# Attention and mixture of experts in one kernel: another written order for the attention stage

## The chip, the cores and the metric

The kernel runs on one NeuronCore of a Trainium2 chip. Five engines matter: PE (TensorE: matmuls and transposes, with PEld its weight loads), DVE (VectorE), ACT (ScalarE), POOL (GpSimd) and SP (SyncE, which here only issues DMAs). Each works through its own list of instructions in order; a DMA is issued by SP or POOL and lands later. The metric is the time of one execution in device microseconds (us); lower is better. A run is timed three times.

## The reference, cut to what matters

Inputs: `q`, `k`, `v` of shape (4 batches, 8 heads, 768 positions, 64), gates of 512 x 8, and eight experts `w1` (512 x 1024) and `w2` (1024 x 512), all float32.

```python
k_sum = k.reshape(B, H, 24, 32, 64).max(axis=3)       # one summary key per 32 positions
v_sum = v.reshape(B, H, 24, 32, 64).mean(axis=3)
scores = [scale * q @ k.T where |i - j| < 16 else -1e9,  scale * q @ k_sum.T + log(32)]
a = softmax(scores);  x = (a @ [v, v_sum]) -> (3072 tokens, 512)
logits = x @ w_gate;  e = argmax(logits)
out[t] = softmax(logits)[e] * sigmoid(x @ w_output_gate)[e] * (relu(x[t] @ w1[e]) @ w2[e])
```

## The kernel before, in words

The first stage is attention, over 24 tiles of 128 positions (6 per batch). The second is the expert stage: tokens of one expert are gathered in slots of 256 and put through two layers of matmuls. Attention is recorded by hand (`tc.manual_schedule` over all five engines): the order in which `attention` calls its helpers is the order on every engine, and the framework only adds semaphore waits. So a wait of one instruction holds up everything written behind it on its engine.

Before the tiles, `load` brings 256 positions of q or k by DMA from SP, `reorder` copies them into another layout, `prep_k` and `prep_q` turn them on PE (`transposed`) and ACT copies them from PSUM into `kt` and `qt`. `load_vw` brings v into `vw`, in windows of 64 positions with a halo, two DMAs per window; `means` and `gather_means` make the block means of v on PE, `put_means` copies them into `vw` on POOL. `k_sum` copies the block maxima `km` into `kt`. `clear` zeroes parts of `kt` and `vw`.

The loop over tiles runs with a lead of `AHEAD` = 2: iteration i writes `scores(i+2)` (PE `sp`, then DVE adds the mask, `pr`), `exps(i+1)` (ACT), `values` and `norm` of the tiles in `at[i]` (PE `pv`, DVE `xs`), `turn_p(i)` (PE `pt`, ACT copies to `pT`), `smallest(i+2)` (DVE `mn`), loads, the work in `todo`, `put_means`, `store_x` (POOL writes `xs` to DRAM), `subtract(i+2)` (POOL) and `turn_x` (PE `xtr`, ACT `xT`). `HELD` = 4 makes `values` begin in iteration 5, two tiles per iteration until they trail by one tile. Once the last tile of a batch is there, `logits` and `turn_logits` (PE `lp`, `lt`) and `route` follow: `route` finds the expert of each token and the place in the list of that expert, and writes the lists with six indirect DMAs from POOL (`l_dr`, one per tile, each behind a small MEMSET `gap`). After batch 1 `early_slots` computes the first three slots, and `fetch_list` and `fetch` gather their lists (`lst`) and tokens (`xg`), also by indirect DMA from POOL. In iterations 18 to 23 `late_work` adds the loading (SP) and splitting (ACT, DVE) of the first expert's weights.

PSUM has eight banks, which the kernel holds as four tags of two: S for scores, PT for `pt`, PV for `pv`, and TR for everything else.

```python
    for i, (b, tok) in enumerate(tiles):
        if i + AHEAD < n:
            scores(i + AHEAD)
        if i + 1 < n:
            exps(i + 1)
        for t in at[i]:
            values(t)
            norm(t)
        turn_p(i)
```

Of the kernel before, what the change touches and what calls it, by code (L numbers as in the profile page):

```python
# [30 lines left out]
BUFS = {"mn": 4, "pr": 3, "pTe": 4, "pTl": 3, "xs": 3, "den": 3, "xT": 2, "ls": 2, "rawk": 3, "rawq": 2, "natk": 2, "natq": 1}  # L31
# [4 lines left out]
HELD = 4  # L36
# [4 lines left out]
WARM = 44  # L41
# [25 lines left out]
C_SUM = C_AVG + 3 * 32  # L67
# [4 lines left out]
def constants():  # L72

    c = np.zeros((P, C_END), np.float32)
    q = np.arange(P)[:, None]
    col = np.arange(W)
    rel = 64 * (q // 64) + np.where(col < LW, col - PAD, col - PAD - NS)[None, :]
    is_sum = ((col >= LW) & (col < LW + NS))[None, :]
    for t in range(3):
        ok = np.abs(q - rel) < 16  # L80
        if t == 1:
            ok &= rel >= 0
        if t == 2:
# [8 lines left out]
    c[:, C_SEL:C_SEL + 2 * E] = p[:, None] % 32 == np.arange(2 * E)[None, :]  # L92
    for m in range(3):
        for half in range(2):
            row = PAD + 32 * half + np.arange(32)
            c[np.where(row < LW, row, row + NS), C_AVG + 32 * m + 2 * m + half] = 1.0 / 32.0
    for j in range(NS):
        c[32 * (j // 6) + j % 6, C_SUM + j] = 1.0
    return c


def body(tc, q, k, v, w_gate, w_ogate, w1, w2, ident, cst, out):
    nc = tc.nc
    with (
# [22 lines left out]
        with tc.manual_schedule(engines=ALL):  # L127
            for event in attention(tc, const, sa, sb, st, ps, dr, q, k, v, id_sb, c_sb, wg_sb, x_dr, l_dr, rt, late_work):
                if event == "routed":
                    moe.add_slots(early_slots(tc, const, c_sb, rt))  # L130
                    for s in range(EARLY):
                        moe.fetch_list(s, 2)
# [4 lines left out]
                else:  # L137
                    tail = event[1]
# [46 lines left out]
def attention(tc, const, sa, sb, st, ps, dr, q, k, v, id_sb, c_sb, wg_sb, x_dr, l_dr, rt, late_work):  # L185
# [6 lines left out]
    def clear(i):  # L192
# [5 lines left out]
        nc.gpsimd.memset(VW[i][LW:LW + NS, :, :, 0:D], 0.0)  # L198

    def evac(dst, src, scale=None, engine="a"):  # L200
        if engine == "v":
            nc.vector.tensor_copy(dst, src)
        else:
            nc.scalar.activation(dst, src, AF.Copy, scale=1.0 if scale is None else scale)

# [20 lines left out]
    def load_vw(b, tok):  # L226
        for blk in (2 * tok, 2 * tok + 1):
            t = VW[b % 2][:, blk]
            lo = PAD if blk == 0 else 0
            n = PAD if blk == NB - 1 else 32  # L230
            s0 = 64 * blk - PAD
            nc.sync.dma_start(t[lo:LW, :, 0:D], v[b, :, s0 + lo:s0 + LW, :].rearrange("h s d -> s h d"))
            nc.sync.dma_start(t[LW + NS:LW + NS + n, :, 0:D], v[b, :, s0 + LW:s0 + LW + n, :].rearrange("h s d -> s h d"))

    def means(b, m):
        if m == 0:
            msp[0] = ps.tile([P, H * D], F32, name=f"ms{b}", tag="TR", bufs=PB["TR"])
        for j in range(4):
            nc.tensor.matmul(msp[0][32 * j:32 * j + 32],
                             lhsT=c_sb[0:W, C_AVG + 32 * m:C_AVG + 32 * m + 32],  # L240
                             rhs=VW[b % 2][:, 3 * j + m, :, 0:D], start=m == 0, stop=m == 2)
        if m == 2:
            evac(MT.rearrange("p h d -> p (h d)"), msp[0])

    def gather_means(b):
        mg = ps.tile([P, H * D], F32, name=f"mg{b}", tag="TR", bufs=PB["TR"])
# [10 lines left out]
    ms, msp, km = {}, [None], {}  # L257
    first_tags = ["TR", "TR", "S", "S", "PT", "PT", "PV", "PV"]

    def transposed(kind, b, u, g):  # L260
        n = nat[kind, b, u]
        tag = first_tags.pop(0) if first_tags else "TR"
        pt = ps.tile([P, 2, 256], F32, name=f"{kind}tr{b}{u}{g}", tag=tag, bufs=PB[tag])
# [35 lines left out]
    def scores(i):  # L299
# [3 lines left out]
        sp = [ps.tile([P, HP, P], F32, name=f"sp{b}{tok}{x}", tag="S", bufs=PB["S"]) for x in range(2)]  # L303
# [28 lines left out]
    def turn_p(i):  # L332
# [5 lines left out]
        for x in range(2):  # L338
            pt = ps.tile([W, HP, P], F32, name=f"pt{b}{tok}{x}", tag="PT", bufs=PB["PT"])
# [4 lines left out]
    def values(i):  # L344
# [3 lines left out]
        for g in range(2):  # L348
            po = ps.tile([P, 4, D + 1], F32, name=f"pv{b}{tok}{g}", tag="PV", bufs=PB["PV"])
# [18 lines left out]
    def store_x(i):  # L368
        b, tok = tiles[i]
        n0 = b * S + tok * P  # L370
        nc.gpsimd.dma_start(x_dr[n0:n0 + P, :], xss[i].rearrange("p h d -> p (h d)"))

    def turn_x(i):
        b, tok = tiles[i]
        xs = xss.pop(i)
        xp = ps.tile([P, NC, P], F32, name=f"xtr{b}{tok}", tag="TR", bufs=PB["TR"])
# [6 lines left out]
    def logits(b, tok):  # L383

        lp = ps.tile([P, 2 * P], F32, name=f"lp{b}{tok}", tag="TR", bufs=PB["TR"])
# [6 lines left out]
    def turn_logits(b, tok):  # L392
        lt = ps.tile([P, 2, 2 * E], F32, name=f"lt{b}{tok}", tag="TR", bufs=PB["TR"])
# [8 lines left out]
    def route(b):  # L402
# [22 lines left out]
        rk = ps.tile([P, TB + 1, E], F32, name=f"rk{b}", tag="TR", bufs=PB["TR"])  # L425
# [3 lines left out]
        tot = ps.tile([P, E], F32, name=f"tot{b}", tag="TR", bufs=PB["TR"])  # L429
# [8 lines left out]
        posi = tmp("posi", [P, TB], I32)  # L438
        nc.vector.tensor_copy(posi, pos)

# [15 lines left out]
        for t in range(TB):  # L456
            nc.gpsimd.memset(rt["gap"], 0.0)
# [9 lines left out]
    def route_to(b):  # L467

        if b not in routes:
            routes[b] = route(b)  # L470
            next(routes[b])
        else:
            for _ in routes[b]:
                pass
# [4 lines left out]
    for s in range(2):  # L479
        load("q", *steps[s])  # L480
    for tok in range(TB):
        load_vw(0, tok)
    for u in range(3):
        load("k", 1, u)
    for u in range(3):
        reorder("k", 0, u, "vav"[u])
        for g in range(2):
            prep_k(0, u, g)
    reorder("q", 0, 0, "a")
    for g in range(2):  # L490
        prep_q(0, 0, g)
    k_sum(0, "v")
    load("q", *steps[2])
    reorder("q", 0, 1, "p")
    load("q", *steps[3])
    for g in range(2):
        prep_q(0, 1, g)
# [12 lines left out]
    todo = {}  # L510

    def later(i, work):
        todo.setdefault(i, []).append(work)

    for b in range(B):
        first = live[TB * b]
        if b == 0:
            later(first - 2, lambda: [means(0, m) for m in range(3)])
            later(first - 1, lambda: gather_means(0))
        else:  # L520
            later(first - 3, lambda b=b: [means(b, m) for m in range(2)])
            later(first - 2, lambda b=b: means(b, 2))
            later(first - 1, lambda b=b: gather_means(b))
    for s in range(2, len(steps)):
        for g in range(2):
            later(2 * s - 4, lambda s=s, g=g: prep_q(*steps[s], g))
    for b in range(1, B):
        for tok, gs in ({1: (0, 1), 2: (2, 3), 3: (4, 5)} if b == 1 else {0: (0,), 1: (1, 2, 3), 2: (4,), 3: (5,)}).items():
            for x in gs:
                later(TB * (b - 1) + tok, lambda b=b, x=x: prep_k(b, x // 2, x % 2))  # L530
# [5 lines left out]
    exps(0)  # L536
    reorder("q", *steps[2], "p")
    load("q", *steps[4])
    for i, (b, tok) in enumerate(tiles):

        if i + AHEAD < n:
            scores(i + AHEAD)
        if i + 1 < n:
            exps(i + 1)
# [7 lines left out]
        if i == 0:  # L552
            clear(1)
        if i % 2 == 1 and (i + 5) // 2 < len(steps):
            reorder("q", *steps[(i + 5) // 2])
            if (i + 9) // 2 < len(steps):
                load("q", *steps[(i + 9) // 2])
        for kb in range(1, B):
            u = {TB * (kb - 1) + x: y for y, x in enumerate((1, 2, 3) if kb == 1 else (-1, 0, 2))}.get(i)
            if u is not None:  # L560
                reorder("k", kb, u)
            for u in {TB * (kb - 2) + 3: (0, 1), TB * (kb - 2) + 4: (2,)}.get(i, ()) if kb > 1 else ():
                load("k", kb, u)
            t = i - (0 if kb == 1 else TB * (kb - 1) - 1)
            if 0 <= t < TB:
                load_vw(kb, t)
        for x in todo.pop(i, []):
            x()
        for t in range(n):
            if live[t] == i + 1:  # L570
                put_means(*tiles[t])
        if tok == 3 and b + 1 < B:
            k_sum(b + 1)
        for t in at[i]:
            store_x(t)
# [12 lines left out]
        if i == live[2 * TB - 1] + 3:  # L588
            yield "routed"
        if i == live[3 * TB - 1]:  # L590
            yield "last batch"
# [3 lines left out]
    for i in sorted(todo):  # L595
        for x in todo[i]:
            x()
    b, tok = tiles[-1]
    yield "tiles done", [lambda: (values(n - 1), norm(n - 1), store_x(n - 1)), lambda: turn_x(n - 1), lambda: logits(b, tok),
                         lambda: (turn_logits(b, tok), route_to(b)), lambda: route_to(b)]  # L600


def slot_tables(tc, const, c_sb, name, n, t, r):
# [9 lines left out]
    while sft < V:  # L613
# [3 lines left out]
        sft *= 2  # L617
    sh = [P, n, V]
# [13 lines left out]
    rowi = tmp("rowi", [P, 2, n], I32)  # L632
    es, esi = tmp("es", [P, n]), tmp("esi", [P, n], I32)
# [11 lines left out]
    return [([rowi[:, t2, s:s + 1] for t2 in range(2)], esi[0:1, s:s + 1]) for s in range(n)], inc, exc  # L645


def early_slots(tc, const, c_sb, rt):
# [8 lines left out]
    slots, inc, exc = slot_tables(tc, const, c_sb, "a", EARLY, t, base)  # L657
# [7 lines left out]
    return slots  # L665
# [23 lines left out]
class Experts:  # L689
# [133 lines left out]
    def start(self, late_work):  # L823

        self.fetch(0, 2)
# [165 lines left out]
```

## Time and profile before

| | us |
|---|---|
| median of three runs (630.93 to 634.79) | 633.65 |
| profiled execution | 635.28 |
| its span, from the first to the last instruction | 633.5 |
| first matmul of tile scores starts | 27.41 |
| first matmul of the expert stage starts | 282.46 |

In the profiled execution the granted clock of PE is 0.883 of full on average; it is 0.78 from 27.40 to 282.46 us and 0.97 behind that. PE is busy for 169.13 us of the 255.06 us between those two points, and for 330.13 us of the 351.04 us after them. The profile is read as follows: a row of the timeline has a start, a busy time, engine and line, operation with output and inputs, the number of instructions, and in brackets how long the engine was idle before and what ended that idle time. Between start and start of two neighbouring rows of one engine lies what the work really took, since PE's rows overlap a little.

### The profile page before, as it was taken

The page shows a single profiled execution, that of the slowest core. Times are in us where ns is not written, and L with a number is a line of the kernel's source. Part 1 is how long each engine was busy: PE and PEld are TensorE (multiplying, and loading weights), DVE is VectorE, ACT ScalarE, POOL GpSimd, SP SyncE. Part 2 cuts the span into 40 slices and gives each one's busy share as a digit, 9 for nine tenths or more (in the row PEclk, how much of TensorE's full clock was granted, in tenths as well). Part 3 has the DMA queues.
Part 4 walks back from the last instruction along what each step waited for, and adds up shares of the span by engine and source line. Part 5 has one row for each costly group of instructions (what it writes and reads, how often), then busy time and mean ns, then how long its engine had stood idle before and what let it go on. Part 6 is the DMA issues. An engine that isn't in the chain of part 4 may idle for free. (4 is left out here: it accounts for less than half of the span.)

```text
span 633.5 us, 12710 instructions
## 1 busy us (share of the span) xinstructions
PE 513.2 (81%) x4368; PEld 428.7 (68%) x4368; DVE 363.6 (57%) x798; ACT 310.0 (49%) x604; POOL 271.4 (43%) x310
## 2 busy tenths in 40 slices
PE   4668777874870796189999999999999999997992
PEld 4456455642660565079888899889889889885661
DVE  4444534462563257358955775675665765764883
ACT  2326425441650255156544664665554655654782
POOL 7085744527634775460477245353441321211111
PEclk7557969995985798589998999999999999997997
DMA  9966755261743013148286674686585584455881
GB/s 234 179 163 133 167 137 116 85 151 30 164 105 76 25 53 120 47 161 298 80 284 209 225 270 152 229 229 234 209 251 208 209 284 168 168 197 186 298 315 66
DMA packets 108563, 109.51 MB, mean 173 GB/s; under 512 B 46238, under 2 KB 70974, under 8 KB 108480
## 3 DMA queue, kind: packets, MB, share of 16 engines
q1 hardware_dynamic: 99344, 88.96, 46.9%
q0 software_dynamic: 9136, 19.56, 9.8%
q8 instruction: 38, 0.62, 0.4%
q14 instruction: 45, 0.37, 0.2%
HBM read 97.51 MB, written 13.59 MB: 175 GB/s over the span
## 5 line engine op out<-in xcount | busy, mean ns | idle before, releaser
L810 PE MATMUL hp<-xhl,w1h 128*128 128x256 f32 x384 | 109.2, 285 | 0.6 <-DVE xhl L794 0.6
L811 PE MATMUL hp<-xhl,w1l 128*128 128x256 f32 x384 | 108.9, 285 | 0.0
L809 PE MATMUL hp<-xhl,w1h 128*128 128x256 f32 x384 | 107.8, 285 | 1.4 <-ACT xhl L793 1.4
L779 ACT ACTIVATE w2h<-raw 128x512 fp32r<-128x512 f32 x104 | 63.9, 630 | 64.2 <-PE yp L905 23.1
L780 DVE TENSOR_TENSOR w2l<-raw,w2h 128x512 fp32r<-128x512 f32 x104 | 69.4, 687 | 38.9 <-ACT w2h L779 33.6
L903 PE MATMUL yp<-w2h,hh 128*128 128x512 f32 x216 | 86.8, 402 | 0.2 <-ACT hh L873 0.2
L904 PE MATMUL yp<-w2l,hh 128*128 128x512 f32 x216 | 85.2, 394 | 0.0
L905 PE MATMUL yp<-w2h,hl 128*128 128x512 f32 x216 | 84.9, 396 | 0.2
L746 POOL DMA_INDIRECT xg<-x_dr,lst x28 | 34.1, 1219 | 105.4 <-PE xp L791 100.1
L809 PEld LDWEIGHTS hp<-xhl,w1h 128*128 128x128 f32 x384 | 73.6, 193 | 3.0 <-ACT xhl L793 1.9
L810 PEld LDWEIGHTS hp<-xhl,w1h 128*128 128x128 f32 x384 | 74.3, 193 | 1.8 <-DVE xhl L794 0.8
L811 PEld LDWEIGHTS hp<-xhl,w1l 128*128 128x128 f32 x384 | 74.3, 194 | 0.0
L780 DVE TENSOR_TENSOR w1l<-raw,w1h 128x512 fp32r<-128x512 f32 x104 | 66.0, 688 | 9.3 <-ACT w1h L779 8.1
L314 DVE TENSOR_TENSOR pr<-sp,c_sb 128x480 f32<-128x480 f32 x48 | 29.3, 652 | 69.2 <-PE sp L309 65.5
L813 DVE SCALAR_TENSOR_TENSOR hl<-hp,hh 128x256 fp32r<-128x256 f32 x96 | 39.5, 421 | 43.4 <-ACT hh L812 43.2
L330 ACT ACTIVATE pr<-pr 128x960 f32<-128x960 f32 x24 | 24.1, 1003 | 79.4 <-POOL pr L326 78.2
L812 ACT ACTIVATE hh<-hp 128x256 fp32r<-128x256 f32 x96 | 36.4, 380 | 52.7 <-PE hp L811 50.6
L352 PE MATMUL pv<-vw,pT 120*64 120x65 f32 x768 | 35.1, 251 | 30.5 <-POOL vw L255 25.0
L779 ACT ACTIVATE w1h<-raw 128x512 fp32r<-128x512 f32 x104 | 57.5, 620 | 4.6 <-PE hp L810 3.9
L352 PEld LDWEIGHTS pv<-vw,pT 120*64 120x64 f32 x768 | 30.9, 162 | 36.1 <-POOL vw L255 27.5
L309 PE MATMUL sp<-kt,qt 64*64 64x120 f32 x768 | 35.8, 334 | 20.2 <-POOL kt L288 18.5
L326 POOL TENSOR_TENSOR pr<-pr,mn 128x960 f32<-128x960 f32 x24 | 42.9, 1788 | 14.1 <-DVE mn L321 13.2
(298 smaller groups left out, 965.0 us busy)
## 6 DMA issues: line engine op xcount, KB each, us to landing
raw<-in_moe_w_dram SPq DMA_DIRECT2D x208, 256.0 KB, 5.2
raw_k<-in_k_dram SPq DMA_DIRECT2D x12, 512.0 KB, 6.0
raw_q<-in_q_dram SPq DMA_DIRECT2D x12, 512.0 KB, 4.4
x_dr<-xs POOLq DMA_DIRECT2D x24, 256.0 KB, 3.8
vw<-in_v_dram SPq DMA_DIRECT2D x44, 128.0 KB, 4.5
vw<-in_v_dram SPq DMA_DIRECT2D x44, 64.0 KB, 4.0
lst<-l_dr,rowib POOLq DMA_INDIRECT x34, 4.3
xg<-x_dr,lst POOLq DMA_INDIRECT x28, 4.6
```

The lines of the kernel that those rows point to most:

```text
L326: nc.gpsimd.tensor_tensor(pr, pr, mns.pop(i).unsqueeze(2).to_broadcast([P, H, W]), ALU.subtract)
L352: nc.tensor.matmul(po[64 * y:64 * y + 64, h % 4, :], lhsT=pT[:, h % 2, h // 2, 64 * y:64 * y + 64], rhs=VW[b % 2][:, 2 * tok + y, h, 0:D + ...
L779: nc.scalar.activation(hi, raw, AF.Copy)
L780: nc.vector.tensor_tensor(lo, raw, hi.bitcast(F32), ALU.subtract)
L809: nc.tensor.matmul(hp, lhsT=w_h[:, fs], rhs=self.xh[:, c, :], start=c == 0, stop=False)
L810: nc.tensor.matmul(hp, lhsT=w_h[:, fs], rhs=self.xl[:, c, :], start=False, stop=False)
L811: nc.tensor.matmul(hp, lhsT=w_l[:, fs], rhs=self.xh[:, c, :], start=False, stop=c == NC - 1)
L812: nc.scalar.activation(hh[:, j, :], hp, AF.Relu)
L813: nc.vector.scalar_tensor_tensor(hl[:, j, :], hp, 0.0, hh[:, j, :].bitcast(F32), ALU.max, ALU.subtract)
L903: nc.tensor.matmul(y, lhsT=hh[:, j, tk], rhs=w_h, start=j == 0, stop=False)
L904: nc.tensor.matmul(y, lhsT=hh[:, j, tk], rhs=w_l, start=False, stop=False)
L905: nc.tensor.matmul(y, lhsT=hl[:, j, tk], rhs=w_h, start=False, stop=j == NF - 1)
```

## The change

Line numbers of the changed kernel are higher by 3 to 27. The parts:

- All uses of PSUM take the next of four tags in turn (`bank`), so the eight banks go round in the order in which they are written.
- `route` is a generator with more stops: three phases, each in an iteration of its own, and then one stop per indirect DMA. For batch 0 one DMA is written per iteration, for batches 1 and 2 three per iteration. `early_slots` is spread over three iterations, and the lists of the first three slots are fetched in iterations 19, 20 and 21 instead of all in one. The tokens of slot 0 are fetched from `late_work`, in iteration 19.
- `HELD` is 2: `values` begins in iteration 3. The means of batch 0 come in iteration 2, and `means` is one call of 13 matmuls instead of three parts of 4.
- `store_x` is issued by SP instead of POOL, at the start of the next iteration.
- `exps(i+1)` is written behind `turn_p(i)` and the work in `todo`.
- k of later batches is reordered by ACT instead of POOL. `clear(1)` moves ahead of the tiles, and the large MEMSET of `vw` shrinks from 12 windows to one. Half of batch 0's `load_vw` DMAs are issued by POOL. Reordering and turning of q is moved by an iteration.

```diff
-BUFS = {"mn": 4, "pr": 3, "pTe": 4, "pTl": 3, "xs": 3, ...
+BUFS = {"mn": 4, "pr": 3, "pTe": 2, "pTl": 3, "xs": 4, ...
-HELD = 4
+HELD = 2
-WARM = 44
+WARM = 64
-        nc.gpsimd.memset(VW[i][LW:LW + NS, :, :, 0:D], 0.0)
+        nc.gpsimd.memset(VW[i][LW:LW + NS, NB - 1, :, 0:D], 0.0)
+    turn = itertools.cycle(("TR", "S", "PT", "PV"))
+    def bank(shape, name):
+        tag = next(turn)
+        return ps.tile(shape, F32, name=name, tag=tag, bufs=PB[tag])
...
-        sp = [ps.tile([P, HP, P], F32, name=f"sp{b}{tok}{x}", tag="S", bufs=PB["S"]) for x in range(2)]
+        sp = [bank([P, HP, P], f"sp{b}{tok}{x}") for x in range(2)]
...
-        nc.gpsimd.dma_start(x_dr[n0:n0 + P, :], xss[i].rearrange("p h d -> p (h d)"))
+        nc.sync.dma_start(x_dr[n0:n0 + P, :], xss.pop(i).rearrange("p h d -> p (h d)"))
...
         for t in range(TB):
+            yield
             nc.gpsimd.memset(rt["gap"], 0.0)
...
-        reorder("k", 0, u, "vav"[u])
+        reorder("k", 0, u, "vap"[u])
...
+    for tok in range(TB):
+        load_vw(0, tok, (1,), nc.gpsimd)
+    reorder("q", *steps[0], "v")
...
     for i, (b, tok) in enumerate(tiles):
+        for t in at[i - 1] if i else ():
+            store_x(t)
         if i + AHEAD < n:
             scores(i + AHEAD)
-        if i + 1 < n:
-            exps(i + 1)
         for t in at[i]:
             values(t)
             norm(t)
         turn_p(i)
...
-        for x in todo.pop(i, []):
+        for x in early.pop(i, []) + todo.pop(i, []):
             x()
+        if i + 1 < n:
+            exps(i + 1)
...
-                reorder("k", kb, u)
+                reorder("k", kb, u, "a")
...
+                later(i + 4, lambda tb=tb: route_to(tb))
+                for x in range(TB):
+                    later(i + 5 + x // (1 if tb == 0 else 3), lambda tb=tb: scatter(tb), put)
-        if i == live[2 * TB - 1] + 3:
-            yield "routed"
+        if live[2 * TB - 1] + 7 <= i < live[2 * TB - 1] + 7 + EARLY:
+            yield "list", i - live[2 * TB - 1] - 7
```

Three places in the written order follow; `pr15` is the score tile of batch 1, tile 5, and the brackets give the semaphores that an instruction waits for (DMASW: a DMA issued by POOL).

POOL before, at the lists of batch 0, behind the subtraction for tile 5 of batch 1 (three of the six DMAs and the rows behind them):

```order
L326 TENSOR_TENSOR pr15_1280<-pr15_1280,mn15_1322 128x960
L457 MEMSET gap_135 128x1
L458 DMA l_dr_75<-pair0_1507,posi0_1493 24704x2 [waits DMASW7_49,DVE_49]
...
L458 DMA l_dr_75<-pair0_1507,posi0_1493 24704x2 [waits DMASW3_49]
L457 MEMSET gap_135 128x1 [waits Pool_49]
L458 DMA l_dr_75<-pair0_1507,posi0_1493 24704x2 [waits DMASW4_49]
L255 COPY vw1_150<-mst1_1062 24x8x64 [waits DMASW3_49,DMASW2_49,DMASW4_49,DMASW1_49,DMASW7_49,DMASW0_49,Pool_49]
L255 COPY vw1_150<-mst1_1062 24x8x64
L371 DMA x_dr_74<-xs13_1424 128x512 [waits DMASW5_49]
L326 TENSOR_TENSOR pr20_1402<-pr20_1402,mn20_1444 128x960 [waits PE_49,Activation_49,Pool_49]
```

POOL in the changed kernel, at the first two of those DMAs, two and three tiles later:

```order
L471 DMA l_dr_75<-pair0_1503,posi0_1395 24704x2 [waits DMASW2_49,DVE_49]
L338 TENSOR_TENSOR pr21_1544<-pr21_1544,mn21_1585 128x960 [waits DVE_49,PE_49,Activation_49]
L236 COPY nat_q22_1702<-raw_q22_1239 128x1024 [waits DMAHW1_49,PE_49]
L269 COPY vw0_169<-mst2_1725 24x8x64 [waits DMASW2_49,Activation_49,Pool_49]
L269 COPY vw0_169<-mst2_1725 24x8x64
L470 MEMSET gap_155 128x1 [waits Pool_49]
L471 DMA l_dr_75<-pair0_1503,posi0_1395 24704x2 [waits DMASW3_49]
L338 TENSOR_TENSOR pr22_1659<-pr22_1659,mn22_1700 128x960 [waits DVE_49]
L269 COPY vw0_169<-mst2_1725 24x8x64 [waits DMASW3_49,Pool_49]
```

The copy into `vw` still waits for the DMA ahead of it, but it is now one DMA, with a subtraction and often a copy of q between, and no store of `xs`.

ACT before, in the iteration of tile 4 of batch 1 and at the start of the next:

```order
L330 ACTIVATE pr15_1280<-pr15_1280 128x960
L204 ACTIVATE pT14_1431<-pt140_1432 120x512
L204 ACTIVATE pT14_1431<-pt141_1438 120x512
L204 ACTIVATE qt1_146<-qtr210_1461 128x512
L204 ACTIVATE qt1_146<-qtr211_1467 128x512
L446 ACTIVATE eo0_1499<-o10_1497 128x6
L204 ACTIVATE xT12_1382<-xtr13_1531 128x4x128
L330 ACTIVATE pr20_1402<-pr20_1402 128x960
```

ACT in the changed kernel, in the iteration of tile 3 of batch 1:

```order
L211 ACTIVATE pT13_1340<-pt130_1341 120x512
L211 ACTIVATE pT13_1340<-pt131_1347 120x512
L211 ACTIVATE qt0_165<-qtr200_1355 128x512
L211 ACTIVATE qt0_165<-qtr201_1361 128x512
L211 ACTIVATE kt0_167<-ktr221_1367 128x2x4x48
L211 ACTIVATE kt0_167<-ktr221_1367 128x2x4x16
L211 ACTIVATE ls11_1402<-lp11_1397 128x256
L342 ACTIVATE pr14_1194<-pr14_1194 128x960
L211 ACTIVATE xT12_1423<-xtr12_1418 128x4x128
```

The exponential of the next tile (`pr`) stood ahead of the copies of this tile's `pT`; it now stands behind them and behind all copies of the iteration but `xT`.

POOL in the changed kernel, in iterations 19 and 20, where the first list, the tokens of slot 0 and the second list are fetched (before, the three lists stood in iteration 15, and the tokens in 18):

```order
L338 TENSOR_TENSOR pr33_2521<-pr33_2521,mn33_2562 128x960 [waits DVE_49,PE_49,Pool_49]
L760 DMA lst0_2594<-l_dr_75,rowia_2233 128x2 x2
L773 DMA xg0_2469<-x_dr_74,lst0_2594 128x512 [waits DMAHW6_49,DMAHW4_49,DMAHW7_49,DMAHW1_49,DMASW6_49]
L773 DMA xg1_2470<-x_dr_74,lst0_2594 128x512 [waits DMASW7_49]
L269 COPY vw1_170<-mst3_2427 24x8x64 [waits DMASW1_49,DMASW0_49,Pool_49]
L269 COPY vw1_170<-mst3_2427 24x8x64
L338 TENSOR_TENSOR pr34_2630<-pr34_2630,mn34_2671 128x960 [waits PE_49,DVE_49,Activation_49,Pool_49]
L760 DMA lst1_2701<-l_dr_75,rowia_2233 128x2 x2
```

The gather of the tokens waits for the landing of the list right ahead of it, and the next copy into `vw` for the landing of the tokens.

More of the change, by code (lines that the diff above doesn't have):

```diff
@@ L383, in logits @@
     def logits(b, tok):
-        lp = ps.tile([P, 2 * P], F32, name=f"lp{b}{tok}", tag="TR", bufs=PB["TR"])
+        lp = bank([P, 2 * P], f"lp{b}{tok}")
         for c in range(NC):
@@ L428, in route @@
             nc.tensor.matmul(rk[:, sft:TB, :], lhsT=rt["ones"], rhs=ohb[:, 0:TB - sft, :], start=False, stop=sft == TB - 1)
-        tot = ps.tile([P, E], F32, name=f"tot{b}", tag="TR", bufs=PB["TR"])
+        tot = bank([P, E], f"tot{b}")
         for t in range(TB):
@@ L470, in route_to, with scatter @@
             routes[b] = route(b)
[L471 to L474, printed above, removed]
+        next(routes[b], None)
+    def scatter(b):
+        next(routes[b], None)
     clear(0)
```

205 lines of the change are left out of this document (109 added, 96 removed).

## The prediction

> **What bounds the kernel now.** I begin with the page's busy tenths in 40 slices (15.8 us each) and the clock of PE under them.
>
> ```profile
> PE   4668777874870796189999999999999999997992
> PEclk7557969995985798589998999999999999997997
> ```
>
> From the eighteenth slice on PE is at 8 or 9 of ten nearly throughout: the expert stage. Before that it falls to 4, 0 and 1. A table of two windows, split at the first expert matmul, puts numbers to it (window, length, then busy time and count of PE, PEld, DVE, ACT, POOL, then clock, DMA share, GB/s).
>
> ```profile
> 27.40:282.46 255.06, 169.13 (x2249) 125.77 (x2249) 119.37 (x317) 99.21 (x188) 142.18 (x185) 0.78 0.44 108
> 282.46:633.50 351.04, 330.13 (x2036) 291.04 (x2036) 233.51 (x466) 201.87 (x399) 116.63 (x105) 0.97 0.64 218
> ```
>
> In the second window PE has 20.9 us free of 351. The change reorders nothing there, so those 351 us stay. In the first, PE is free for 85.9 us and no other engine is busier than PE: the limit is the written order, that is, waits. The waits of that window (engine, line, what it waited for, us in total, times, longest):
>
> ```profile
> PE pv L352 <- POOL vw L255: 25.0, 5, 12.8
> PE sp L309 <- POOL kt L288: 18.5, 2, 17.4
> PE pv L352 <- DVE xs L366: 5.2, 4, 1.7
> PE ktr L267 <- POOL nat_k L223: 5.0, 1, 5.0
> PE lp L387 <- DVE at L433: 4.3, 1, 4.3
> PE ms L239 <- DMA vw<-in_v_dram: 2.5, 1, 2.5
> PE lp L387 <- ACT qt L204: 0.2, 1, 0.2
> ```
>
> The two largest come from three places, which the timeline shows.
>
> ```profile
> 151.45 1.16 POOL L255 COPY vw<-mst 24x512 f32<-24x512 f32 x2 [3.21 <-DMA l_dr<-pair,posi]
> 152.11 2.55 PE L352 MATMUL pv<-vw,pT 120*64 120x65 f32 x32 [8.68 <-POOL vw L255]
> 206.54 1.16 POOL L255 COPY vw<-mst 24x512 f32<-24x512 f32 x2 [7.04 <-DMA l_dr<-pair,posi]
> 208.24 1.88 PE L309 MATMUL sp<-kt,qt 64*64 64x120 f32 x32 [17.39 <-POOL kt L288]
> 269.59 1.16 POOL L255 COPY vw<-mst 24x512 f32<-24x512 f32 x2 [4.27 <-DMA l_dr<-pair,posi]
> 270.24 2.55 PE L352 MATMUL pv<-vw,pT 120*64 120x65 f32 x32 [12.84 <-POOL vw L255]
> ```
>
> Each time the six indirect DMAs of `route` have just stood on POOL, the copy into `vw` waits for their landing, and PE waits for what is written behind: 8.68 + 17.39 + 12.84 = 38.9 us.
>
> **The change, part by part.** First the floor: PE's work at full clock, from rows of an undisturbed stretch and one row of the means.
>
> ```profile
> 59.70 2.78 PE L239 MATMUL ms<-vw,c_sb 120*32 120x512 f32 x24
> ...
> 227.37 1.05 PE L309 MATMUL sp<-kt,qt 64*64 64x120 f32 x32
> 228.35 1.15 PE L352 MATMUL pv<-vw,pT 120*64 120x65 f32 x32
> 229.43 1.09 PE L341 MATMUL pt<-id_sb,pr 128*120 128x128 f32 x8
> 230.45 1.05 PE L247 MATMUL mg<-mt,c_sb 128*32 128x512 f32 x2
> 231.43 1.41 PE L267 MATMUL qtr<-id_sb,nat_q 128*128 128x128 f32 x8
> 232.80 0.62 PE L395 MATMUL lt<-c_sb,ls 128*128 128x16 f32 x4
> ...
> 237.19 0.64 PE L387 MATMUL lp<-xT,wg_sb 128*32 128x256 f32 x8
> 237.76 0.66 PE L378 MATMUL xtr<-id_sb,xs 128*128 128x128 f32 x4
> 238.34 1.05 PE L309 MATMUL sp<-kt,qt 64*64 64x120 f32 x32
> ```
>
> Per tile 1.05 + 1.15 + 1.09 + 0.66 = 3.95, by 24: 94.8. The turns of q: 11 x 1.41 = 15.5; those of k have half the transposes: 18 x 0.705 = 12.7. `lp` and `lt` 12 x 1.26 = 15.1; the means 4 x (2.78 x 13/12 = 3.0) = 12.0; `mg` 4 x 1.05 = 4.2. Together 154.3. Rows overlap: the eleven from 227.37 to 238.34 fill 10.97 us and add up to 11.62, so the factor is 0.944: 145.7, with the small matmuls of routing **147 us**. Measured busy time is 169.1, so 22 us are PE at less than full clock, and the other 86 are waits.
>
> *Routing in phases* takes the 38.9. Between a scatter and the copy that waits for it there now lies POOL work of another kind:
>
> ```profile
> L326 POOL TENSOR_TENSOR pr<-pr,mn 128x960 f32<-128x960 f32 x24 | 42.9, 1788 | 14.1 <-DVE mn L321 13.2
> L458 POOL DMA_INDIRECT l_dr<-pair,posi x18 | 17.9, 993 | 28.1 <-DVE lg L202 8.8 <-DVE pair L455 8.6 <-DVE ti_early L655 7.8
> L371 POOL DMA_DIRECT2D x_dr<-xs x23 | 13.0, 565 | 21.1 <-DVE xs L366 20.7 <-issue 0.4
> L223 POOL COPY nat_k<-raw_k 128x1024 f32<-128x1024 f32 x9 | 9.3, 1035 | 0.0
> ```
>
> A scatter still costs 0.99 us of issue and then a landing of 3.2 to 7.0 (mean 4.84), of which a subtraction (1.79) and often more is cover; some 3 us stay per wait, on POOL and not yet on PE. The values trail the scores by three tiles instead of one or two, so PE has other tiles to go on with.
>
> *Banks in turn.* A matmul that waits for an evacuation of something it does not read waits for its bank: `lp` for `at` (4.3) down to `lp` for `qt` (0.2). I count nineteen such groups of `lp`, `lt`, `ktr`, `qtr`, `xtr`, `rk` and `tot` in that list, 24.3 us together; eight banks until reuse instead of two should take most: 20. Bounds: 0, should each wait pass on to the next instruction, and 24.
>
> *Stores to SP, k to ACT.* POOL loses 13.0 us of issues, the waits for `xs` under them (20.7) and the copies of k, with them PE's 5.0 for `nat_k`. POOL's own work falls from 142 to some 115 (13.0 of stores, 9.3 of copies of k, 5.2 of the memset of the second `vw`). On SP a store stands ahead of loads that are written an iteration or more before use; if that cover goes, a store that waits for `xs` delays a load by what `xs` lacks, at most the 1.7 of one wait above.
>
> *Exponentials behind the turn of p.* ACT does what PE waits for first; then `exps(i+1)` has a bit over an iteration for its subtraction instead of about half. In PE's rows this is worth little of its own, up to the 5.2 for `xs`; I count 0 and keep 5 either way.
>
> *The start.* A POOL memset of 5.21 us goes, and with it the stretching of the DVE copy beside it, 4.50 against 0.68 for the same copy later; a turn of q moves behind the first scores.
>
> ```profile
> 5.02 5.21 POOL L198 MEMSET vw<- 24x6144 f32 x1
> 6.29 4.50 DVE L223 COPY nat_k<-raw_k 128x1024 f32<-128x1024 f32 x1 [5.26 <-DMA raw_k<-in_k_dram]
> 17.80 0.68 DVE L223 COPY nat_k<-raw_k 128x1024 f32<-128x1024 f32 x1
> 25.51 1.97 PE L267 MATMUL qtr<-id_sb,nat_q 128*128 128x128 f32 x8 [1.33 <-POOL nat_q L223]
> 27.41 1.88 PE L309 MATMUL sp<-kt,qt 64*64 64x120 f32 x32
> ```
>
> 27.41 - 3.82 - 1.90 = 21.7; the third copy of k, from DVE to POOL, no longer stands behind two reductions, an estimated 1.7 more: scores start at **20**. Bounds: 25.5, if only the turn goes, and 19.
>
> *What the change adds.* Between the last turn of k of a batch (tile 3 of the batch before) and its first scores (an iteration later) stand the maxima and POOL's `k_sum`, as today; today that costs PE 18.5 - 17.39 = 1.1 us, with shorter iterations an estimated 2 at each of three batch boundaries: 5 more. And the three lists and the tokens of slot 0 in iterations 19 to 21: each is a gather whose landing POOL waits for directly, with nothing between, some 3.2 to 7.0 by the rows of the scatters; four of them, 13 to 28 on POOL, of which three tiles of lead hide most: **4** on PE, bounds 0 and 20.
>
> **The sum.** Idle: 85.9 - 38.9 - 5.0 - 20 + 5 = **27**; 11 if every smaller wait goes too (the waits for `xs`, `vw` by DMA and the small ones on operands are about 16), 50 if the banks give nothing and the added waits cost 3 more. Clock: of the 22 us lost, the stretch right behind the start is the part that I expect to remain (PE has half clock from 15 to 30 us, 0.50 with 9.18 us busy of 15): **9** for the first 18 us; bounds 4 and 15. So the expert stage starts at 20 + 147 + 27 + 9 + 4 = **207** instead of 282.46, and the time is 207 + 351.0 + 1.8 (635.28 less the span of 633.5) = **560 us**. Low: 19 + 147 + 11 + 4 = 181, 534. High, with the lists at 0 because their high end is the first rival's: 25.5 + 147 + 50 + 15 = 237.5, 590. The profiled execution is 0.26% over the median of 633.65, too little to correct for.
>
> **The clock, weighed against a rule.** The windows in question:
>
> ```profile
> 15.00:30.00 15.00, 9.18 (x63) 7.28 (x61) 4.90 (x11) 5.97 (x13) 1.03 (x1) 0.50 0.90 167
> 60.00:75.00 15.00, 10.64 (x146) 5.87 (x139) 7.51 (x14) 6.12 (x13) 7.55 (x11) 1.00 0.86 196
> ```
>
> With PE busy for 9.18 of 15 us the clock was 0.50, with 10.64 of 15 it was 1.00: the border lies near there, though the first of the two is also the stretch in which PE begins. I expect some 156 us busy of 187, 0.83. The Trainium skill, in "TensorE: Matmul & The Clock Gate", section "A second HAM failure mode: psum-queue depth-cycling", says that cycling through PSUM banks each iteration made PE pause so often and so briefly that its clock swung between half and full. That speaks against this change. No run here shows banks in rotation; by that rule the clock term would be many times 9, which the second rival prices from rows.
>
> **Rivals.** *POOL stays the limit* (0.15). For it: POOL has 115 us of work left, and up to twelve landings now stand alone in its queue (six of batch 0, two of batch 1, three lists, one gather of tokens), at some 3 us each 36 us more, 151 of 187, and ACT waits for POOL's subtractions at each tile. Against it: 36 us of slack and three tiles of lead. If half of the landings reach PE, beyond the 4 counted, some 18 to 20 us are added: 579, with 575 to 590.
>
> *PE's clock* (0.05; slower). The price is the floor by the share h of PE's work done at half clock: 20 + 147 x (1 + h) + 31 of waits. Today h is 22/147 = 0.15; the start of the expert stage passes 282.46 from h = 0.58 on, and at 0.8 it is 316: 668 us. Against it: today's undisturbed stretches show 9 in the clock row with the same chains, and the change takes away the long gaps.
>
> *The order is not the limit* (0.17): only the three stalls and the start improve, and the smaller waits pass on to whatever is next, since bank, operand and copy come late together. 635.3 - 38.9 - 7.4 = 589. For it: nine different tiles are named as what those small waits waited for, so no single one is the cause. A fourth case, that the three stalls are merely cut into pieces as long (no change, within 8 of 634), gets 0.03: PE idles in long blocks now because values have no other tile to go on with.
>
> **How the numbers follow.** The forecast has 0.60: 560, its own range 534 to 590 by the bounds, most of it in 542 to 580. Rivals: 579 (0.15), 589 (0.17), no change (0.03), 668 (0.05). A range from 540 to 594 leaves out the last two, some 4 in 100 of the forecast below 540 and a little of the third. Faster by over 1% (what a measurement of this kernel can tell from no change): 0.92; within it 0.03; slower 0.05.
>
> **What would show it.** In the profile of the changed kernel: first scores at 19 to 22; the expert stage starting between 185 and 225 and lasting 351 to within 3; no single wait of PE over 6 us; waits of `lp`, `ktr`, `qtr` and `xtr` for foreign evacuations under 6 us in sum; PE busy 150 to 162 at a clock of 0.9. It is wrong if waits of PE for `kt`, `vw` or `pr` from POOL add up to over 30 (first rival), if the clock stays under 0.7 (second), if the sum of small waits stays at 40 (third), or if the expert stage itself grows, because a list or the weights of slot 0 come late for an attention stage that ends 75 us sooner.

## The result, and the profile after

The changed kernel takes 564.59 us (median of four runs, 559.14 to 569.25) against 632.44: a ratio of 0.8895, 95% interval 0.8822 to 0.8969. The forecast was 560, in a range of 540 to 594. The profiled execution is the slowest of the four (569.25, span 567.5, mean clock 0.926 where the others have 0.938 to 0.940), so its stages together are some 5 us longer than those of the median.

The page's slices of 14.2 us each, which answer to those of before:

```profile
PE   6679999896895667999999999999999999979990
PEclk9777999999797667899999999999999999988996
```

The holes of 4, 0 and 1 are gone. What is left of low digits is the start, a 6 in slice ten, and the slices thirteen to sixteen, the end of attention and the beginning of the expert stage. The two windows, split at the first scores and at the first expert matmul (columns as before the change):

```profile
17.33:212.86 195.53, 159.04 (x2266) 118.09 (x2265) 121.12 (x314) 106.44 (x199) 115.11 (x139) 0.86 0.62 148
212.86:567.50 354.64, 330.08 (x2039) 292.59 (x2037) 234.21 (x468) 202.93 (x399) 123.51 (x116) 0.96 0.67 216
```

PE's matmuls in the attention stage are nearly the same, its free time falls from 85.9 to 36.5 us, POOL's busy time from 142 to 115. By stage, predicted and measured:

| | before | predicted | after |
|---|---|---|---|
| first scores | 27.41 | 20 | 17.33 |
| PE busy, attention | 169.1 | 147 + 9 | 159.0 |
| PE free, attention | 85.9 | 27 + 4 | 36.5 |
| expert stage | 351.0 | 351.0 | 354.6 |
| span | 633.5 | 558.2 | 567.5 |

The waits of PE in the attention stage, all groups:

```profile
PE pv L364 <- POOL vw L269: 17.5, 11, 7.7
PE sp L321 <- POOL kt L300: 6.9, 3, 5.4
PE sp L321 <- ACT qt L211: 4.3, 2, 3.9
PE ktr L279 <- ACT nat_k L234: 2.5, 1, 2.5
PE xtr L390 <- DVE xs L378: 2.3, 2, 1.3
PE pt L353 <- ACT pr L342: 1.8, 2, 0.9
PE ms L253 <- DVE pr L326: 0.5, 1, 0.5
PE qtr L279 <- DVE lg L209: 0.2, 1, 0.2
```

Of the nineteen groups that the prediction counted as waits for a bank (24.3 us: a matmul waits for a tile that it does not read), one is left, `qtr` for `lg` with 0.2 us; `ms` for `pr`, 0.5 us, is new. The other rows are waits for operands. At the start the copy that took 4.50 us takes 0.69, and the first turn of k takes 1.09 us:

```profile
6.85 0.69 DVE L236 COPY nat_k<-raw_k 128x1024 f32<-128x1024 f32 x1 [5.82 <-DMA raw_k<-in_k_dram]
7.60 1.09 PE L279 MATMUL ktr<-id_sb,nat_k 128*128 128x128 f32 x8 [0.72 <-DVE nat_k L236]
17.33 1.88 PE L321 MATMUL sp<-kt,qt 64*64 64x120 f32 x32
```

### The profile page after: what moved, and what is told of

Same layout as the page of the kernel before. It is cut to its first block, busy times and chain, and to the rows that moved or that the text cites. A ratio compares the mean times of both kernels' runs of the same rounds, so it can differ in the third digit from the quotient of the medians.

```text
span 567.5 us, 12812 instructions
## 1 busy us (share of the span) xinstructions
PE 500.6 (88%) x4396; PEld 420.8 (74%) x4396; DVE 362.1 (64%) x798; ACT 315.9 (56%) x613; POOL 252.8 (45%) x289
## 4 chain that ended last, share of the span: by engine, by line
PE 54%; DMA 17%; issue 12%; DVE 5%; POOL 4%; SPq 3%; ACT 3%; POOLq 0%; ACTq 0%; DVEq 0%
PE hp L836 6%; PE hp L838 6%; PE hp L837 6%; PE yp L931 6%; PE yp L930 6%; PE yp L932 6%; DMA out_dram<-y,lst 5%; PE pv L364 3%; DMA l_dr<-pair,posi 3%; PE pt L353 2%; PE ms L253 2%; DMA xg<-x_dr,lst 2%; DMA raw_k<-in_k_dram 2%; SPq L247 2%; DMA raw<-in_moe_w_dram 2%
## 5 line engine op out<-in xcount | busy, mean ns | idle before, releaser
L836 PE MATMUL hp<-xhl,w1h 128*128 128x256 f32 x384 | 110.0, 287 | 0.5 <-DVE hl L840 0.5
L837 PE MATMUL hp<-xhl,w1h 128*128 128x256 f32 x384 | 109.6, 286 | 0.0
L773 POOL DMA_INDIRECT xg<-x_dr,lst x28 | 36.0, 1284 | 115.3 <-PE xp L818 108.5
L930 PE MATMUL yp<-w2h,hh 128*128 128x512 f32 x216 | 85.9, 398 | 0.1
L807 DVE TENSOR_TENSOR w1l<-raw,w1h 128x512 fp32r<-128x512 f32 x104 | 67.6, 704 | 9.9 <-ACT w1h L806 9.0
L211 ACT ACTIVATE pT<-pt 120x512 f32<-120x512 f32 x48 | 26.7, 595 | 50.1 <-PE pt L353 48.8
L338 POOL TENSOR_TENSOR pr<-pr,mn 128x960 f32<-128x960 f32 x24 | 43.2, 1802 | 13.9 <-DVE mn L333 11.7
L269 POOL COPY vw<-mst 24x512 f32<-24x512 f32 x48 | 28.8, 629 | 45.6 <-ACT mst L211 28.0
L932 PEld LDWEIGHTS yp<-w2h,hl 128*128 128x128 f32 x216 | 40.6, 188 | 9.1 <-DVE hl L901 0.8
L364 PEld LDWEIGHTS pv<-vw,pT 120*64 120x64 f32 x768 | 29.3, 152 | 23.4 <-POOL vw L269 21.1
```

Source lines behind the costliest of these rows:

```text
L338: nc.gpsimd.tensor_tensor(pr, pr, mns.pop(i).unsqueeze(2).to_broadcast([P, H, W]), ALU.subtract)
L364: nc.tensor.matmul(po[64 * y:64 * y + 64, h % 4, :], lhsT=pT[:, h % 2, h // 2, 64 * y:64 * y + 64], rhs=VW[b % 2][:, 2 * tok + y, h, 0:D + ...
L807: nc.vector.tensor_tensor(lo, raw, hi.bitcast(F32), ALU.subtract)
L836: nc.tensor.matmul(hp, lhsT=w_h[:, fs], rhs=self.xh[:, c, :], start=c == 0, stop=False)
L837: nc.tensor.matmul(hp, lhsT=w_h[:, fs], rhs=self.xl[:, c, :], start=False, stop=False)
L930: nc.tensor.matmul(y, lhsT=hh[:, j, tk], rhs=w_h, start=j == 0, stop=False)
```

## Experiments

**Banks, undone.** The changed kernel with own tags:

```diff
-        tag = next(turn)
+        tag = first_tags.pop(0) if first_tags else own.get(name[:2], "TR")
```

> The changed kernel with each use of PSUM in its own tag of two banks again (S, PT, PV, TR), all else as changed. Theory (the written order is the limit, and the bank waits are a term of it): waits of lp, ktr, qtr, xtr for foreign evacuations come back with 15 to 24 us, 580 to 589 us in place of 564.6. Rival (small waits only pass on from one instruction to the next): under 570. Should the rotation cost clock, the clock of the attention stage rises here above the 0.86 of the changed kernel.

578.45 us (573.83 to 581.25), ratio to before 0.911 (0.906 to 0.916): 13.9 us more, a little under the theory's window and far from the rival's. Waits for foreign evacuations are back, in this kernel's waits for example:

```profile
PE ktr L280 <- ACT qt L211: 5.8, 6, 3.8
PE mg L262 <- DVE km L294: 3.2, 3, 1.2
PE tot L444 <- DVE km L294: 2.7, 2, 1.3
PE lt L408 <- DVE km L294: 2.5, 2, 1.2
```

The clock of the stage is 0.90 here, above the 0.86 of the changed kernel's profile; but other kernels with rotating banks below have 0.81 to 0.91, and the kernel before has 0.78 without and 0.79 with rotation, so no cost of rotation can be read from it.

**Scatters at once, in the changed kernel.**

```diff
-                    later(i + 5 + x // (1 if tb == 0 else 3), lambda tb=tb: scatter(tb), put)
+                    later(i + 5, lambda tb=tb: scatter(tb), put)
```

> The changed kernel with the six scatters of a batch written in one iteration, as before; all else as changed. Theory (spreading them is what takes the three stalls away): three blocks of some 12 us return on POOL, of which the lead of three tiles hides a part; 575 to 600 us. Rival (the lead of the values hides them anyway, spread or not): under 570.

560.97 us (552.43 to 561.74; no interval was formed): not slower than the changed kernel. The theory falls. POOL issues six scatters (the indirect DMAs of `route`) in a row, and the next copy into `vw` comes 4.6 us after the last issue ended, with no landing to wait for:

```profile
115.01 0.97 POOL L471 DMA_INDIRECT l_dr<-pair,posi  x1 [0.19 <-issue]
120.60 1.16 POOL L269 COPY vw<-mst 24x512 f32<-24x512 f32 x2 [1.79 <-ACT mst L211]
```

So spreading them over iterations brings nothing here. What covers the landings is still in place: behind the last scatter stand a subtraction and a copy of q, 2.8 us of POOL's work. A look back at the kernel before shows what was overlooked: a wait of POOL ahead of its first scatter, longer than the six issues that follow (7.5 us).

```profile
131.84 0.12 POOL L457 MEMSET gap<- 128x1 f32 x1
137.90 0.21 DVE L433 TENSOR_TENSOR at<-rk,base 128x48 f32<-128x48 f32 x1 [2.32 <-PE rk L428]
140.80 1.05 POOL L458 DMA_INDIRECT l_dr<-pair,posi  x1 [8.83 <-DVE lg L202]
```

The scatter stood in the same iteration as the vector work of `route` whose result it writes. That work took only some 2.6 of the 8.83 us, from 137.90 on: most of the wait passed before its matmul `rk` had its turn on PE. New theory: the phases matter, not the spreading.

**Rotation alone, in the kernel before** (`bank` for all uses in attention).

> The kernel before with PSUM in rotation alone. Theory (the bank waits are a term of their own, worth 20 us): 608 to 617 us against 632.4. Rival (they pass on): 626 to 634. The means of v hold a bank over two iterations here, which in rotation may cost a few us.

617.76 us (616.93 to 619.81), ratio 0.976 (0.973 to 0.980): 15 us, just outside the theory's window. Its waits show that the rival was half right:

```profile
PE pv L357 <- POOL vw L262: 34.0, 8, 15.2
PE sp L314 <- POOL kt L293: 20.9, 2, 19.4
PE ms L246 <- DMA vw<-in_v_dram: 8.6, 2, 4.5
27.40:265.99 238.59, 158.85 (x2249) 120.83 (x2249) 118.15 (x313) 96.66 (x187) 142.49 (x185) 0.79 0.48 117
```

The bank waits are down to 2.2 us (`lp` and `tot` for `pr`), but those for `vw` and `kt` grow from 43.5 to 54.9 and that for the DMA of v from 2.5 to 8.6: PE's free time falls only from 85.9 to 79.7. The rest is PE's busy time, 169.1 to 158.9 us for the same matmuls; why it fell at nearly the same mean clock was not settled.

**The copy into `vw` by ACT, in the kernel before.**

```diff
-            nc.gpsimd.tensor_copy(VW[b % 2][LW:LW + NS, blk, :, 0:D], ms[b][LW:LW + NS])
+            nc.scalar.activation(VW[b % 2][LW:LW + NS, blk, :, 0:D], ms[b][LW:LW + NS], AF.Copy)
```

> The kernel before with one edit: the copy of the means into vw by ACT instead of POOL, which then waits for no scatter. Theory (the three stalls are waits for landings, taken over from the copy): the 38.9 us shrink to the 7.7 us of issue per six scatters, less what the lead hides: 595 to 612 us. Rival (the six issues hold POOL's queue, the landing is not the point): 620 or more.

618.29 us (617.52 to 619.96), ratio 0.977 (0.974 to 0.980): 14.6 us, between the two. With the copy on ACT it carries no wait for a scatter, and the second and third stall shrink, but they don't go; at the first, PE now waits 5.36 us for another copy of ACT:

```profile
192.94 1.88 PE L309 MATMUL sp<-kt,qt 64*64 64x120 f32 x32 [9.09 <-POOL kt L288]
257.85 2.51 PE L352 MATMUL pv<-vw,pT 120*64 120x65 f32 x32 [6.89 <-ACT vw L255]
```

By size the 14.6 us are what POOL waited for landings in the kernel before (14.5 us, shown below). That the landings alone are their price is not shown, since the copy has also left POOL's queue with its issues and its wait ahead of them. That wait is still there, 31.0 us over three batches, and it reaches ACT: ahead of the last stall ACT's exponential waited 7.86 us for POOL's subtraction, and the copy into `vw` stood behind it.

**Scatters one iteration later, in the kernel before.**

```diff
+        yield
         for t in range(TB):
             nc.gpsimd.memset(rt["gap"], 0.0)
...
                 later(i + 3, lambda tb=tb: route_to(tb))
+                later(i + 4, lambda tb=tb: route_to(tb))
```

> The kernel before with one edit: the six scatters of a batch (still all at once) are written one iteration behind the vector work of route whose result they write, and the fetch of the lists with them. Theory (each stall is mostly POOL's wait ahead of the first scatter, 8.8 + 8.6 + 7.8 us for DVE, which stands in a row of the profile before): these waits go and PE gets 15 to 25 us: 608 to 618 us against 632.9. Rival (what holds POOL is the issue and the landing): over 626.

625.86 us (620.62 to 628.33, ten runs), ratio 0.986 (0.982 to 0.991): 9 us of 634.99, less than 2%, and at the rival's edge. POOL's idle time ahead of the scatters fell from 28.1 to 8.6 us, and the three stalls of PE from 38.9 to 19.2:

```profile
L460 POOL DMA_INDIRECT l_dr<-pair,posi x18 | 18.1, 1003 | 8.6 <-issue 2.9 <-DVE pair L456 2.2 <-DVE lg L203 2.0
202.47 2.55 PE L353 MATMUL pv<-vw,pT 120*64 120x65 f32 x32 [4.58 <-POOL vw L256]
215.07 2.55 PE L353 MATMUL pv<-vw,pT 120*64 120x65 f32 x32 [4.54 <-POOL vw L256]
262.68 2.55 PE L353 MATMUL pv<-vw,pT 120*64 120x65 f32 x32 [10.09 <-POOL vw L256]
```

The mechanism is there: PE's free time in the stage fell by 15 us. But half of that went elsewhere, as PE's busy time in the stage rose by 4 us and the expert stage by 4. The waits of the copy into `vw` for landings stayed as they were, 14.8 us against 14.5.

**Phases joined, in the changed kernel.**

```diff
-                later(i + 3, lambda tb=tb: route_to(tb))
-                later(i + 4, lambda tb=tb: route_to(tb))
-                for x in range(TB):
-                    later(i + 5 + x // (1 if tb == 0 else 3), lambda tb=tb: scatter(tb), put)
+                later(i + 3, lambda tb=tb: [route_to(tb) for _ in range(TB + 2)])
```

> The changed kernel with the last two phases of route and its six scatters in one iteration, as before; all else as changed. Theory (the wait of POOL for DVE ahead of the scatters): 8 to 10 us of wait return three times on POOL, 15 to 30 us on PE: 576 to 592 us. Rival (rotation of the banks and a POOL without stores take the stalls up): under 570.

586.21 us (581.92 to 588.02), ratio 0.926 (0.918 to 0.934): 21.6 us more than the changed kernel, as the theory has it. POOL's wait ahead of the scatters is back (3.5 us in the changed kernel), and with it three stalls of the old kind:

```profile
L471 POOL DMA_INDIRECT l_dr<-pair,posi x18 | 17.8, 991 | 21.3 <-DVE pair L467 10.6 <-DVE ti_early L676 7.9 <-issue 2.9
113.06 1.88 PE L321 MATMUL sp<-kt,qt 64*64 64x120 f32 x32 [14.94 <-POOL kt L300]
165.40 1.88 PE L321 MATMUL sp<-kt,qt 64*64 64x120 f32 x32 [14.70 <-POOL kt L300]
222.54 2.55 PE L364 MATMUL pv<-vw,pT 120*64 120x65 f32 x32 [14.89 <-POOL vw L269]
```

Beside the second experiment this places the effect in the routing: six scatters at once cost nothing as long as their data are ready when POOL comes to them, and they stand where the changed kernel has them. For the edit undoes two things. The changed kernel writes its scatters behind the copies into `vw` of the same iteration; here, as in the kernel before, they stand ahead of these copies and of `k_sum`. At the third stall POOL's wait ahead of the scatters was short:

```profile
209.65 1.00 POOL L471 DMA_INDIRECT l_dr<-pair,posi  x1 [2.78 <-DVE pair L467]
```

The rest of it is the six issues and a wait of 4.67 us for a landing, with the copy behind them. How the 21.6 us divide between the phases and this place was not tried. They are also a balance: the attention stage took 25.8 us more than in the changed kernel's profile, the expert stage 7.4 less.

**Exponentials in front, and stores on POOL, in the changed kernel** (one edit each: `exps(i + 1)` ahead of `values`; `store_x` by POOL, ahead of `subtract`).

> The changed kernel with exps(i+1) in front of values again. Theory (counted at 0, kept at 5 either way): 560 to 570 us. Rival (ACT's order matters, since exps waits for POOL's subtraction and holds up the copies of pT behind it): PE waits for the evacuations of pt and the time is over 575.

565.74 us (563.2 to 571.7), ratio 0.893 (0.885 to 0.901).

> The changed kernel with the stores of x issued by POOL again, ahead of the subtraction. Theory (POOL's queue costs where it waits for xs: 20.7 us of such waits and 13 of issue before): some of it reaches PE, 568 to 580 us. Rival (POOL has slack now): under 566.

564.98 us (563.71 to 567.19), ratio 0.896 (0.889 to 0.903). Neither moves the time. For the stores that is the rival's case: POOL is busy for 128 us of 192 with them, so there is room for them.

**Banks and phases undone together.**

> The changed kernel with both undone: own banks, and the last two phases of route joined with its scatters. Theory (the two are separate terms: 13.9 for the banks and some 22 for the phases, each from its own undoing against 564.6): 597 to 604 us, and what is then left of the gain is the start and the smaller parts. Rival (each covers for the other: with one undone, the other took up part of it): over 608.

600.3 us (598.57 to 601.21), ratio 0.949 (0.945 to 0.953): 35.7 us over the changed kernel, and 13.9 + 21.6 = 35.5. The two are separate terms, as the theory has it. The remaining 33 us to the kernel before lie, by the stages of the two profiles, in the first scores (27.41 to 16.45), PE's free time (85.9 to 74.6), PE's busy time (169.1 to 158.1) and the expert stage (351.0 to 347.7); which edit gives which was not tried.

**Aimed at a better version.** First, the scatters at once, `k_sum` by DVE and the copy into `vw` by ACT, then by DVE.

> Aimed at a better version: the changed kernel with the scatters at once, the copy of the means into vw by ACT, and k_sum by DVE, so that no copy that PE waits for stands in POOL's queue. Theory (PE's waits for vw and kt, 17.5 and 6.9 us in the changed kernel, are waits for POOL's queue): 540 to 555 us. Rival (ACT, with 27 us of copies more, is late with pT and qt in place of them): 560 to 570.

580.17 us (575.51 to 583.62), ratio 0.916 (0.909 to 0.923). Worse than even the rival said; ACT's queue is now what PE waits for, 31 times:

```profile
PE pv L364 <- ACT vw L269: 28.5, 31, 2.9
```

> As the version with the copy by ACT, but both copies by DVE. Theory: 540 to 555 us. Rival (DVE's reductions for mn and the divisions of x are late in place of them): 560 to 570.

568.48 us (567.4 to 574.44), ratio 0.9005 (0.894 to 0.907): the rival's case and no gain; the waits only move to other queues.

```profile
PE sp L321 <- DVE kt L300: 9.5, 3, 4.1
PE pv L364 <- DVE vw L269: 7.2, 7, 2.7
PE pv L364 <- ACT w1h L806: 6.0, 2, 3.7
```

This points not to the queue as such, but to its worst stretch. PE's waits in the changed kernel from 178 us on, and the last 30 us of the stage:

```profile
PE pv L364 <- POOL vw L269: 13.1, 5, 7.7
182.86:212.86 30.00, 18.01 (x205) 14.17 (x205) 13.58 (x42) 10.89 (x20) 16.29 (x20) 0.66 0.37 98
```

Here POOL's copies stand behind the fetches of lists and tokens; the longest waited for the landing of the tokens:

```profile
187.36 1.16 POOL L269 COPY vw<-mst 24x512 f32<-24x512 f32 x2 [4.58 <-DMA xg<-x_dr,lst]
188.01 2.56 PE L364 MATMUL pv<-vw,pT 120*64 120x65 f32 x32 [7.66 <-POOL vw L269]
```

The last run moves the copies of the last batch alone.

```diff
-            nc.gpsimd.tensor_copy(VW[b % 2][LW:LW + NS, blk, :, 0:D], ms[b][LW:LW + NS])
+            (nc.vector if b == B - 1 else nc.gpsimd).tensor_copy(VW[b % 2][LW:LW + NS, blk, :, 0:D], ms[b][LW:LW + NS])
```

> The changed kernel with one edit: for the last batch alone the copy of the means into vw is DVE's, so that it does not stand behind the fetches of the lists and tokens on POOL. Theory (the list stage costs 13.1 us of PE's waits for vw behind 178 us, with a clock of 0.66 there, against the 4 us that were predicted): those waits go and the time falls by 8 to 14 us, to 550 to 557. Rival (the weights of the first expert come late and PE waits for them, as for w1h and w2h, in place of vw): within 4 us of 564.6.

552.19 us (545.51 to 556.49), ratio 0.868 (0.861 to 0.874): 12.4 us under the changed kernel, in the theory's window, and faster than the two versions above. In its waits from 170 us to the expert stage the 13.1 have become 2.0 (2.4 over a stretch as long as in the changed kernel), with 2.2 behind a weight and 3.2 for other work of ACT, and the stage takes 180.5 instead of 195.5 us. Of these 15 us, 7.4 are PE's free time and 7.6 its busy time:

```profile
PE pv L364 <- ACT w1h L806: 2.2, 1, 2.2
PE pv L364 <- DVE vw L269: 2.0, 1, 2.0
16.50:197.03 180.53, 151.46 (x2265) 115.61 (x2265) 132.07 (x325) 106.24 (x201) 109.24 (x128) 0.91 0.69 159
```

## Why the prediction was right, and where its steps were wrong

The forecast was 560 and the median is 564.6. The frame held: the bound was the written order, PE's free time in the attention stage was what could be had, and the floor of 147 us was not reached (the rows that give its factor of 0.944 are twelve, not eleven; the factor is right). By its steps:

- *Routing in phases takes the 38.9.* Right in the place, incomplete in the mechanism, and too large: undone, it costs 21.6. The prediction said that POOL's other work between a scatter and the copy would cover the landing, and that values trail the scores by three tiles instead of one or two. The first is so in part: the copy's waits for landings fell by half, and with all six scatters at once it waited for none. The second misread the loop: once `HELD` tiles are caught up, both kernels write `scores(i+2)` and the values of tile i-1 in one iteration. What it left out is larger on POOL: the vector work of `route` now lies iterations ahead of the scatters. The 28.1 us that POOL idled for it stood in a row that the prediction quoted for the price of the scatter and did not read to the end; 3.5 are left. The copy into `vw`, before and after:

```profile
L255 POOL COPY vw<-mst 24x512 f32<-24x512 f32 x48 | 27.7, 606 | 37.4 <-ACT mst L204 18.2 <-DMA l_dr<-pair,posi 14.5 <-DMA xg<-x_dr,lst 2.5
L269 POOL COPY vw<-mst 24x512 f32<-24x512 f32 x48 | 28.8, 629 | 45.6 <-ACT mst L211 28.0 <-DMA l_dr<-pair,posi 7.7 <-DMA lst<-l_dr,rowia 4.7
```

- *Banks in turn, 20.* As waits 24.3 became 0.7; undone they cost 13.9, alone they bring 15. Some of those waits do pass on, as the third rival had it.
- *Exponentials and stores, 0 on PE.* Right, both within a percent of the changed kernel. The 5.0 us for `nat_k`, which were to go with k on ACT, became 2.5.
- *The start, 7.4.* 10.1. The first two turns of k took 1.09 instead of 1.97 us and the third 1.57, which was not counted; this kernel also has 64 warming matmuls instead of 44, and whether these did it was not tried.
- *`k_sum`, 5 more.* `sp` waits 6.9 for `kt`, against the 1.1 counted from before: 5.8.
- *The lists, 4.* Far too small, though within its bounds of 0 and 20: 13.1 us of waits behind 178 us in this profile, 9.5 and 10.4 over the same stretch with the exponentials in front and with the stores on POOL, and 12.4 us of time by the last run. The landings there are direct waits of POOL, as the prediction said; the lead was too short to hide them.
- *Clock, 9.* 159.0 - 147 = 12. The border that the prediction read from two windows, between 9.18 and 10.64 us busy of 15, does not hold in the same trace:

```profile
30.00:45.00 15.00, 12.33 (x120) 9.74 (x120) 8.52 (x11) 4.17 (x6) 10.49 (x9) 0.50 0.83 207
```

- *The expert stage stays.* It grew by 3.6 in the profile, and by 2.9 and 1.6 with the exponentials in front and with the stores on POOL. Its first 20 us hold 16.85 us of PE's work at a clock of 0.74, where before 20.00 stood at 1.00, and ACT waits for weights (windows of before and after, and rows of after):

```profile
282.46:302.46 20.00, 20.00 (x153) 18.05 (x154) 17.80 (x48) 14.12 (x31) 3.05 (x3) 1.00 0.91 317
```

```profile
212.86:232.86 20.00, 16.85 (x117) 15.11 (x116) 11.95 (x34) 9.61 (x21) 6.31 (x14) 0.74 0.72 177
ACT w2h L806 <- DMA raw<-in_moe_w_dram: 7.1, 3, 3.5
219.19 0.63 ACT L806 ACTIVATE w2h<-raw 128x512 fp32r<-128x512 f32 x1 [3.37 <-DMA raw<-in_moe_w_dram]
220.35 1.03 PE L399 MATMUL lp<-xT,wg_sb 128*32 128x256 f32 x8 [2.08 <-ACT xT L211]
```

ACT's copy `xT` stands right behind that wait for a weight, and PE waits 2.08 us for it: the late weight that the prediction named last. It does not account for all of the growth, and with the stores on POOL the clock of these 20 us was 1.00.

So the number is nearer than its parts, and in part by luck. By the undoing, phases and banks gave 35.7 us where 38.9 + 20 were counted, 23 too few; all the rest gave some 33, where the 75 us of the forecast leave 16, and which edits gave these is open. Against the profiled 569.25 the start came out 2.7 better, PE's free time 5.5 worse (the lists 9.1 worse, all other waits 23.4 in place of 27), PE's clock 3 and the expert stage 3.6 worse, 9.4 together; and that execution is 4.7 above the median.

Of the signs that the prediction set, these came: the start of the expert stage (212.86), the waits for foreign evacuations, and PE's busy time (159.0). These did not: the first scores (17.33, earlier than 19), the longest wait (7.7, over 6), the clock of 0.9 (0.86), and the expert stage, which grew by more than 3 in this profile.

Of the rivals, *POOL stays the limit* is true mainly of the last 35 us, with 13.1 of PE's 24.4 us of waits for POOL; the 24.4 are under the 30 at which it would have held. *PE's clock* did not happen. With eight banks in rotation:

```profile
60.00:90.00 30.00, 30.00 (x503) 22.13 (x496) 18.84 (x49) 20.18 (x38) 18.43 (x21) 1.00 0.52 132
```

Thirty microseconds without a pause and at full clock. The Trainium skill ("TensorE: Matmul & The Clock Gate", section "A second HAM failure mode: psum-queue depth-cycling") tells of a kernel that cycled through PSUM banks, where PE paused briefly so often that its clock swung. This case does not show it: here rotation took short pauses away, and the low clock, 0.66 and 0.74, stands where PE waits for copies. *The order is not the limit* (589) fell with the phases and the banks, which together are 35.7 us.

## What to carry to other kernels

Where an engine works strictly in order, look at what it waited for ahead of a slow instruction as well as behind it: an instruction whose data are made in the same iteration holds the queue for the whole chain. Writing it later gained 9 us (less than 2%) in the kernel before, and undoing it, together with its place behind the copies, cost 21.6 in the changed one. Then look for the one stretch in which a helper engine's queue is full, and move away only what others wait for there: the same copy moved to another engine everywhere (with `k_sum`, and the scatters at once) gave nothing or lost 16 us, moved for the last batch alone it gave 12. Shared banks in rotation remove waits for foreign evacuations, but part of these only uncover the next wait.

## What the runs showed of the hardware

A copy of 24 x 512 elements takes POOL some 0.6 us, and in the kernel before with the copy on ACT 48 of them took ACT 27.0 us, as long. Yet the changed kernel with them on ACT (and `k_sum` on DVE, and the scatters at once) was 16 us slower, and PE waited 28.5 us for them; what a copy costs depended on its place in a queue. And PE's busy time in the attention stage, for nearly the same matmuls, lay between 151.5 us (last run, mean clock 0.91) and 173.2 us (scatters later, 0.82), so an edit that takes waits away moves this time too, and not always down. The mean clock alone does not tell it, since 158.9 us stood at 0.79 (rotation alone); this was left open.
